# Moving a quarter of the columns of wq's last 64 rows to 64 partitions and eight DMA engines

## The chip, the cores and the metric

The kernel runs on one core of a Trainium2 chip. The metric is the device time of one execution in microseconds (us). The kernel before was timed three times: 210.89, 211.00 and 211.11 us, a median of 211.0 us. A core has five engines that work side by side and wait for each other through semaphores: TensorE (PE: matmuls, and PEld: its weight loads), VectorE (DVE), ScalarE (ACT), GpSimd (POOL) and SyncE (SP). Transfers between the memory of the chip and the core's own memory (128 partitions) are carried by 16 DMA engines. SP, ACT and POOL issue them, each in the order of its own instruction stream.

## The reference: one decode step of attention beside a small MLP

Four sequences (B = 4), one token each, width D = 576. The input x is normalized to xn, and the result is x + A(xn) + B(xn):

```python
q = (x @ wq).reshape(B, Sq, Hq, Dh)             # x [4, 576], wq [576, 4096]: 32 heads of 128
k = k_cache[:, :, Sk - W:, :]                   # 16 kv heads, the last W = 2048 of 8192 positions
v = v_cache[:, :, Sk - W:, :]
p = softmax(q k^T * Dh ** -0.5);  A = (p v).reshape(B, 4096) @ wo            # wo [4096, 576]
x1 = x + hs                                     # hs: gelu(layernorm(x) @ w1), shifted in time, @ w2
B = x1 + gelu(layernorm(x1) @ w3) @ w4          # w3 [576, 4608], w4 [4608, 576]
```

Everything is bfloat16. With a sequence length of 1 every shift of the block with w1 and w2 moves the only token out and a zero in, so hs is zero and the kernel reads neither w1 nor w2. What has to be read is large: the windows of K and V are 32 MiB each, wq, wo, w3 and w4 together some 19 MiB. The arithmetic on it is small, since there are only four tokens.

## The kernel before

**Loads.** The work is cut into eight pairs of kv heads (NPR = 8). For a pair t there is one load of K and one of V, each 128 partitions by 32,768 bytes (4 MiB), issued from POOL (`load_kv`, L125). Three buffers (NKV = 3) hold K and V; a load is issued when the previous user of its buffer is done (`free_one`). Between them POOL issues the four quarters of wo (`load_wo`, L147), w3 in two parts (L152 and L153) and, behind the last V, w4 in six parts (L163), of which the last two are one row of 1,152 bytes per partition. All weights of wq, w3 and w4 share one buffer (tag "w").

**wq.** Its 576 rows are split at 512 (KJ = 4 times 128). The first 512 rows lie four to a partition: `wq_main`, 32,768 bytes on each partition, issued by SP in L143. The last 64 rows lie half a row to a partition: row r is cut into its two halves of 2,048 columns, which go to partitions 2r and 2r + 1, 4,096 bytes on each. SP issues this load first, in L142. ACT issues the load of x (L139), 4 rows of 1,152 bytes. These three are the only loads that SP and ACT issue; everything else is issued by POOL.

**q.** `layernorm` makes xn on four partitions, and `transposed` turns it so that the contracted dimension lies on the partitions: four PE transposes give xnT[:, 0:4] for the first 512 rows. For the last 64 rows POOL first copies the 64 columns of xn into a zeroed tile `dup` (L277 the memset, L279 the copies), once at the even and once at the odd places, and two PE transposes (L284) give xnT[:, 4] and xnT[:, 5], in which every other partition is zero. DVE copies all of it out (L285). So a matmul over 128 partitions with xnT[:, 4 + e] picks half e of the last 64 rows. `q_mm(r, g, j)` (L355) is one such matmul, 512 columns wide, into 32 rows of one of two PSUM tiles; there are 2 x 4 x 5 = 40. The last eight (j = KJ) read the last 64 rows.

**Order.** The schedule is written by hand: each engine works through its instructions in the order in which the program names them. On POOL the issues of the first two K loads (`start_loads`) stand behind the constants, the last of which are sel_jb (L319) and same_j (L329). They need sel_j from DVE (L317), which stands on DVE behind the copy of xnT (L285). On ACT the load of x is followed by a table load and the clearing of xnT, ln2T and qz (`cleared`, L211). Later the loop over pairs mixes scores (L411), softmax and the products with V (L475); at the end PE takes w4 in the order in which it lands (L230, L252), DVE and ACT write out the sum, and SP stores it (L716).

Of the kernel before, what the change touches and what calls it, by code (L numbers as in the profile page):

```python
# [11 lines left out]
BF16 = mybir.dt.bfloat16  # L12
# [10 lines left out]
def kernel(  # L23
# [14 lines left out]
    nc = tc.nc  # L38
    P = 128
    B, Sq, D = A_x.shape  # L40
# [6 lines left out]
    KJ = 4  # L47
    NQ = Hq * Dh
# [4 lines left out]
    QD = 32  # L53
# [8 lines left out]
    NW = SC * QD  # L62
# [15 lines left out]
    wp = ctx.enter_context(tc.tile_pool(name="w", bufs=1))  # L78
# [5 lines left out]
    small = ctx.enter_context(tc.tile_pool(name="small", bufs=2))  # L84
    ps_s = ctx.enter_context(tc.tile_pool(name="ps_s", bufs=3, space=PSUM))
    ps_o = ctx.enter_context(tc.tile_pool(name="ps_o", bufs=2, space=PSUM))
    ps_m = ctx.enter_context(tc.tile_pool(name="ps_m", bufs=2, space=PSUM))
# [49 lines left out]

    x_bf = part(D, B)
    nc.scalar.dma_start(out=x_bf[:], in_=x2)  # L139
    wq_sb = wp.tile([P, KJ * NQ + NQ // 2], BF16, tag="w", name="wq_sb")  # L140
    wq_main = A_wq[0:KJ * P, :].rearrange("(p j) n -> p (j n)", j=KJ)
    nc.sync.dma_start(out=wq_sb[:, KJ * NQ:], in_=A_wq[KJ * P:D, :].rearrange("r (e f) -> (r e) f", e=2))  # L142
    nc.sync.dma_start(out=wq_sb[:, 0:KJ * NQ], in_=wq_main)  # L143

    def load_wo(p):
# [61 lines left out]
    def cleared(shape, name):  # L207
        t = const.tile(shape, BF16, name=name)
        flat = t[:] if len(shape) == 2 else t[:].rearrange("p a b -> p (a b)")
        flat = flat.bitcast(F32)  # L210
        nc.scalar.activation(out=flat, in_=zero[:].bitcast(F32).to_broadcast(list(flat.shape)), func=ACT.Copy)  # L211
        return t

    xnT = cleared([P, KJ + 2, QD], "xnT")
    ln2T = cleared([P, KJ + 2, QD], "ln2T")
    ZP = (NSL - 1) * NJ
    qz = cleared([P, ZP + NPR * 4 * P], "qz")
# [55 lines left out]
                                    op0=ALU.subtract, op1=ALU.mult)  # L273

    def transposed(src_bf, T):
        dup = small.tile([B, 2, P], BF16, tag="dup")
        nc.gpsimd.memset(dup[:], 0.0)  # L277
        for e in range(2):
            nc.gpsimd.tensor_copy(out=dup[:, e, e:P:2], in_=src_bf[:, KJ * P:D])  # L279
        tp = ps_m.tile([P, KJ + 2, B], BF16, tag="m", name="tp")  # L280
        for j in range(KJ):
            nc.tensor.transpose(out=tp[:, j, :], in_=src_bf[:, j:KJ * P:KJ], identity=ident_bf[0:B, 0:B])
        for e in range(2):
            nc.tensor.transpose(out=tp[:, KJ + e, :], in_=dup[:, e, :], identity=ident_bf[0:B, 0:B])  # L284
        nc.vector.tensor_copy(out=T[:, :, 0:B], in_=tp[:])  # L285

    xn_f = part(2 * D, B).bitcast(F32)
    xn_bf = part(D, B)
    layernorm(xn_f, xn_bf, x_bf)
    transposed(xn_bf, xnT)  # L290

    kts = {}
# [9 lines left out]
    for kb in range(NQD):  # L302
        nc.gpsimd.tensor_copy(out=sel[:, :, :, kb, :],
                              in_=ident_bf[:].rearrange("p (ib i e) -> p ib e i", ib=2, e=2))
# [23 lines left out]
    for g in range(2):  # L328
        nc.gpsimd.tensor_copy(out=same_j[:, g * 2 * QD:(g + 1) * 2 * QD].rearrange("p (e s j) -> p e s j", e=2, j=NJ),  # L329
                              in_=sel_j[:].unsqueeze(2).to_broadcast([P, 2, NSL, NJ]))  # L330
# [13 lines left out]
    ln2_bf = part(D, B)  # L344
    layernorm(None, ln2_bf, xn_bf)
    transposed(ln2_bf, ln2T)
    flush_loads()


    q_ps = [ps_s.tile([P, NW], F32, tag="S", name="q_ps") for _ in range(2)]  # L350

    def q_mm(r, g, j):
        c = r * NQD + g
        col, k = (j * NQ + c * NW, j) if j < KJ else (KJ * NQ + g * NW, KJ + r)
        nc.tensor.matmul(out=q_ps[r][g * QD:(g + 1) * QD, :], lhsT=xnT[:, k, :], rhs=wq_sb[:, col:col + NW],  # L355
                         start=(j == 0), stop=False, skip_group_check=True)

    for jr in ((0, 1), (2, 3), (KJ,)):
        for r in range(2):
            for j in jr:  # L360
                for g in range(NQD):
                    q_mm(r, g, j)
# [9 lines left out]
    for r in range(2):  # L372
        nc.vector.tensor_copy(out=q_bf[:, r],  # L373
                              in_=qT_ps[:, r].rearrange("p u (g x) -> p g u x", g=NQD)[:, :, :, 0:B])
    qs_ps = ps_m.tile([P, Hkv, 4, rep, B], F32, tag="m", name="qs_ps")
    for ie in range(4):
        ib, e = divmod(ie, 2)
        nc.tensor.matmul(out=qs_ps[:, :, ie], lhsT=sel[:, ib, e].rearrange("p k i -> p (k i)"),
                         rhs=q_bf.rearrange("p r g u b -> p (r g u b)"), start=True, stop=True)
    for kb in range(NQD):  # L380
        rows = slice(kb * QD, (kb + 1) * QD)
# [365 lines left out]
```

## Time and profile before

| what | value |
|---|---|
| three runs | 210.89, 211.00, 211.11 us |
| the profiled execution's own time | 211.11 us |
| its span, first to last instruction | 209.3 us |
| PE, DVE, ACT, POOL busy | 144.9, 124.8, 29.7, 31.6 us |
| moved by DMA | 87.32 MB in 4,155 packets, 417 GB/s |
| wq main rows: issue to landing | 13.8 us |
| wq last 64 rows: issue to landing | 3.3 us |

The span is what the profiler saw between the first and the last instruction of the core; 1.8 us of the execution lie around it. A "landing" is the moment at which the last part of a transfer has arrived and its semaphore is complete. The trace also holds every DMA packet with its start, its duration, its size and its queue; it does not say on which of the 16 engines a packet ran. Queue q0 is POOL's, q1 is SP's, q10 is ACT's, q8 and q14 bring instructions.

### The profile page before, as it was taken

The numbers are of one execution on the slowest core, as the hardware profiler recorded it, in microseconds if no ns is written. First come the engines' busy times: TensorE is split into PE (matmuls) and PEld (weight loads), VectorE is DVE, ScalarE is ACT, GpSimd is POOL, SyncE is SP. The second block draws the span as 40 slices with busy tenths as digits, with TensorE's granted clock in tenths as the row PEclk, the third lists the DMA queues.
The fourth block names the chain that finished last, engine by engine and source line by source line (L and its number), as shares of the span: only waits on it lengthen the run. The fifth ranks groups of instructions, "written<-read, shape, count | busy, mean of one in ns | idle before, by whom it ended". The sixth has DMA issues, their size and how long they took to land.

```text
span 209.3 us, 2197 instructions
## 1 busy us (share of the span) xinstructions
PE 144.9 (69%) x894; PEld 58.4 (28%) x894; DVE 124.8 (60%) x177; ACT 29.7 (14%) x61; POOL 31.6 (15%) x63
## 2 busy tenths in 40 slices
PE   0249199649679943059996894687957937996954
PEld 0013033222215310014442431143314311443432
DVE  5410779994189700097928990989089818987110
ACT  6402500110102011003001201020002010203100
POOL 5680001003200110000133011001010161100000
PEclk9999859996957995558999999597999996997899
DMA  7999999999999999999999999999999999999991
GB/s 301 401 463 438 401 463 423 438 401 451 451 396 437 447 416 413 392 441 482 413 404 465 432 407 409 477 432 407 457 438 404 446 445 413 438 451 401 419 403 70
DMA packets 4155, 87.32 MB, mean 417 GB/s; under 512 B 488, under 2 KB 496, under 8 KB 1200
## 3 DMA queue, kind: packets, MB, share of 16 engines
q0 software_dynamic: 3840, 82.45, 91.8%
q1 hardware_dynamic: 296, 4.72, 5.4%
q8 instruction: 7, 0.11, 0.2%
q14 instruction: 4, 0.03, 0.0%
q10 hardware_dynamic: 8, 0.00, 0.0%
HBM read 87.17 MB, written 0.00 MB: 416 GB/s over the span
## 4 chain that ended last, share of the span: by engine, by line
DMA 62%; PE 18%; DVE 14%; POOL 2%; issue 2%; ACT 0%; POOLq 0%; DVEq 0%
DMA kn<-in_A_k_cache_dram,row 46%; DMA w_sb<-in_B_w_dram 16%; PE S L411 11%; DVE kt L297 9%; PE O L475 6%; DVE pt L456 1%; POOL w_sb L163 1%; DVE mx L417 1%; PE sum L252 1%; POOL vn L125 0%; PE oT L486 0%; DVE on L496 0%; POOL rstd L268 0%; POOL wo_sb L147 0%; DVE row L116 0%
## 5 line engine op out<-in xcount | busy, mean ns | idle before, releaser
L411 PE MATMUL S<-kt,qz 128*128 128x512 bf16 x256 | 78.4, 439 | 33.4 <-DVE kt L297 33.4
L297 DVE STREAM_TRANSPOSE kt<-kn 128x2048 int32<-128x2048 int32 x32 | 73.7, 2307 | 46.5 <-DMA kn<-in_A_k_cache_dram,row 44.2
L411 PEld LDWEIGHTS <-qz 128*128 128x128 bf16 x256 | 23.4, 104 | 72.6 <-issue 55.8
L475 PE MATMUL O<-vn,pt 128*64 128x512 bf16 x256 | 36.0, 412 | 5.5 <-DVE kt L297 2.5
L456 DVE STREAM_TRANSPOSE pt<-E 64x512 bf16<-64x512 bf16 x32 | 22.1, 690 | 1.2 <-ACT E L447 0.9
L447 ACT ACTIVATE E<-S,bias 128x512 bf16<-128x512 f32 x16 | 10.9, 683 | 75.6 <-DVE bias L440 75.6
L125 POOL DMA_INDIRECT vn<-in_A_v_cache_dram,row x8 | 7.7, 961 | 91.6 <-DVE kt L297 87.5
L475 PEld LDWEIGHTS <-pt 128*64 128x64 bf16 x256 | 13.5, 116 | 22.5 <-issue 13.8
L480 ACT ACTIVATE O_sb<-O,rd 128x512 f32<-128x512 f32 x8 | 5.5, 687 | 62.5 <-PE O L475 62.5
L125 POOL DMA_INDIRECT kn<-in_A_k_cache_dram,row x8 | 7.9, 989 | 42.4 <-PE O L475 23.2
L417 DVE TENSOR_REDUCE mx<-S 128x1 f32<-128x512 f32 x16 | 10.7, 668 | 0.1
L538 PE MATMUL g_ps<-w_sb,ln2T 128*32 128x512 bf16 (+1 forms) x50 | 5.2, 486 | 2.9 <-DMA w_sb<-in_B_w_dram 2.9
L399 PE MATMUL S<-negbig,ohT 4*128 4x512 bf16 x16 | 6.4, 398 | 0.0
L486 PE MATMUL oT<-ident_w,O_sb 128*128 128x128 f32 x32 | 5.2, 286 | 0.0
L355 PE MATMUL q_ps<-wq_sb,xnT 128*32 128x512 bf16 x40 | 4.5, 631 | 0.9 <-DMA wq_sb<-in_A_wq_dram 0.9
L496 DVE TENSOR_REDUCE on<-oT 128x16 bf16<-128x128 f32 x8 | 2.3, 287 | 4.4 <-PE oT L486 4.2
L486 PEld LDWEIGHTS oT<-ident_w,O_sb 128*128 128x128 f32 x32 | 4.1, 149 | 2.2 <-issue 0.9
L163 POOL DMA_DIRECT2D w_sb<-in_B_w_dram x6 | 3.3, 585 | 8.2 <-DMA vn<-in_A_v_cache_dram,row 8.2
L440 DVE TENSOR_SCALAR bias<-bp 128x1 f32<-128x1 f32 x8 | 1.3, 158 | 5.2 <-PE bp L435 5.2
L713 DVE CAST fin<-sum 4x288 bf16<-4x288 f32 x1 | 0.4, 446 | 6.5 <-PE sum L252 6.5
L420 DVE TENSOR_SCALAR dm<-sel_g,mx 128x8 bf16<-128x8 bf16 x16 | 3.9, 243 | 0.6
L373 DVE COPY first<-qT_ps 128x64 bf16<-128x64 bf16 x2 | 0.3, 186 | 6.6 <-PE qT_ps L370 6.6
(103 smaller groups left out, 83.1 us busy)
## 6 DMA issues: line engine op xcount, KB each, us to landing
wo_sb<-in_A_wo_dram POOLq DMA_DIRECT2D x4, 1152.0 KB, 23.6
w_sb<-in_B_w_dram POOLq DMA_DIRECT2D x1, 4608.0 KB, 29.5
wq_sb<-in_A_wq_dram SPq DMA_DIRECT2D x1, 4096.0 KB, 13.8
w_sb<-in_B_w_dram POOLq DMA_DIRECT2D x1, 2592.0 KB, 29.1
w_sb<-in_B_w_dram POOLq DMA_DIRECT2D x2, 576.0 KB, 31.7
w_sb<-in_B_w_dram POOLq DMA_DIRECT2D x1, 1008.0 KB, 31.0
w_sb<-in_B_w_dram POOLq DMA_DIRECT2D x1, 720.0 KB, 32.2
wq_sb<-in_A_wq_dram SPq DMA_DIRECT2D x1, 512.0 KB, 3.3
```

The source lines that it names most:

```text
L125: nc.gpsimd.indirect_dma_start(tl[:].rearrange("p c d -> p (c d)"), None, k_rows if kind == "K" else v_rows, bass.IndirectOffsetOnAxis(ap= ...
L163: nc.gpsimd.dma_start(out=t[:, lo:hi, :], in_=src[e][:, at:at + hi - lo, :])
L297: nc.vector.transpose(out=kt[:], in_=src)
L399: nc.tensor.matmul(out=S_ps[t, u][:].rearrange("p (c k) -> p c k", k=QD), lhsT=ohT[:], rhs=negbig[:].unsqueeze(1).to_broadcast([B, SC, QD] ...
L411: nc.tensor.matmul(out=S_ps[t, u][:], lhsT=qz[:, z0:z0 + P], rhs=kt[:, ib, sl * SC:(sl + 1) * SC, e:2 * QD:2].rearrange("p c k -> p (c k)" ...
L417: nc.vector.reduce_max(out=mx[:], in_=S_ps[t, u][:], axis=AX.X)
L447: nc.scalar.activation(out=E[t, u][:].rearrange("p c k -> p (c k)"), in_=S_ps.pop((t, u))[:], func=ACT.Exp, scale=scale, bias=st["bias", t ...
L456: nc.vector.transpose(out=pts[t % 2 * NU + u][rows, :, e * QD:(e + 1) * QD], in_=e_in[rows])
L475: nc.tensor.matmul(out=O_ps[t][rows], lhsT=pts[t % 2 * NU + u][:, c, :], rhs=vn[:, u, :, c, :], start=(u == 0 and c < 2), stop=False, skip ...
L480: nc.scalar.activation(out=O_sb[t][:], in_=O_ps.pop(t)[:], func=ACT.Copy, scale=st.pop(("rd", t))[:, 0:1])
L486: nc.tensor.transpose(out=oT[:, s, :], in_=o[:, s, :], identity=ident_w[:, s * NJ:s * NJ + P])
L538: nc.tensor.matmul(out=g_ps[g * QD:(g + 1) * QD], lhsT=ln2T[:, k, :], rhs=cols[:, :, i0:i0 + n], start=(j == 0), stop=False, skip_group_ch ...
```

## The change

The four column blocks of 512 in each half row are named by g = 0 to 3. The change takes block g = 0 of both halves, a quarter of the columns of the last 64 rows, out of SP's load. SP's load then has 3,072 bytes on each of the 128 partitions. ACT issues four more loads behind that of x: for each of two blocks of 32 rows (h) and each half (e), 32 partitions by 512 columns (1,024 bytes on a partition). They go to partitions 0 to 63, one row to a partition, so that the two matmuls with g = 0 contract over 64 partitions in place of 128. Within a block, row 8q + g' (q = 0 to 3, g' = 0 to 7) goes to partition 4g' + q, so the outermost dimension of the load has eight steps. xn's 64 columns are put in the same order by a third copy into `dup`, and a third transpose makes xnT[:, 6]. The second use of `transposed` (ln2T) keeps two copies. The tile of wq grows from 18,432 to 18,944 columns, below the 20,736 of w3 and w4 in the same buffer.

```diff
-    wq_sb = wp.tile([P, KJ * NQ + NQ // 2], BF16, tag="w", name="wq_sb")
+    QL = P // 2
+    QT = KJ * NQ
+    QW = NQ // 2 - NW
+    wq_sb = wp.tile([P, QT + QW + 2 * NW], BF16, tag="w", name="wq_sb")
     wq_main = A_wq[0:KJ * P, :].rearrange("(p j) n -> p (j n)", j=KJ)
-    nc.sync.dma_start(out=wq_sb[:, KJ * NQ:], in_=A_wq[KJ * P:D, :].rearrange("r (e f) -> (r e) f", e=2))
+    nc.sync.dma_start(out=wq_sb[:, QT:QT + QW], in_=A_wq[KJ * P:D, :].rearrange("r (e f) -> (r e) f", e=2)[:, NW:])
+    for h in range(2):
+        rows = A_wq[KJ * P + h * QL // 2:KJ * P + (h + 1) * QL // 2, :].rearrange("(q g) n -> g q n", q=4)
+        for e in range(2):
+            nc.scalar.dma_start(out=wq_sb[h * QL // 2:(h + 1) * QL // 2, QT + QW + e * NW:QT + QW + (e + 1) * NW],
+                                in_=rows[:, :, e * NQ // 2:e * NQ // 2 + NW])
     nc.sync.dma_start(out=wq_sb[:, 0:KJ * NQ], in_=wq_main)
...
-    xnT = cleared([P, KJ + 2, QD], "xnT")
+    xnT = cleared([P, KJ + 3, QD], "xnT")
...
     def transposed(src_bf, T):
-        dup = small.tile([B, 2, P], BF16, tag="dup")
+        n = T.shape[1] - KJ
+        dup = small.tile([B, n, P], BF16, tag="dup")
         nc.gpsimd.memset(dup[:], 0.0)
+        if n > 2:
+            nc.gpsimd.tensor_copy(out=dup[:, 2, 0:QL].rearrange("b (h g q) -> b h g q", h=2, q=4),
+                                  in_=src_bf[:, KJ * P:D].rearrange("b (h q g) -> b h g q", h=2, q=4))
...
-        for e in range(2):
+        for e in range(n):
             nc.tensor.transpose(out=tp[:, KJ + e, :], in_=dup[:, e, :], identity=ident_bf[0:B, 0:B])
...
-        col, k = (j * NQ + c * NW, j) if j < KJ else (KJ * NQ + g * NW, KJ + r)
-        nc.tensor.matmul(out=q_ps[r][g * QD:(g + 1) * QD, :], lhsT=xnT[:, k, :], rhs=wq_sb[:, col:col + NW],
+        col, k, rows = (j * NQ + c * NW, j, P) if j < KJ else (QT + (g - 1) * NW, KJ + r, P)
+        if j == KJ and g == 0:
+            col, k, rows = QT + QW + r * NW, KJ + 2, QL
+        nc.tensor.matmul(out=q_ps[r][g * QD:(g + 1) * QD, :], lhsT=xnT[0:rows, k, :], rhs=wq_sb[0:rows, col:col + NW],
                          start=(j == 0), stop=False, skip_group_check=True)
```

More of the change, by code (lines that the diff above doesn't have):

```diff
@@ L275, in transposed @@
     def transposed(src_bf, T):
-        dup = small.tile([B, 2, P], BF16, tag="dup")
+        n = T.shape[1] - KJ
+        dup = small.tile([B, n, P], BF16, tag="dup")
         nc.gpsimd.memset(dup[:], 0.0)
+        if n > 2:
+            nc.gpsimd.tensor_copy(out=dup[:, 2, 0:QL].rearrange("b (h g q) -> b h g q", h=2, q=4),
+                                  in_=src_bf[:, KJ * P:D].rearrange("b (h q g) -> b h g q", h=2, q=4))
         for e in range(2):
             nc.gpsimd.tensor_copy(out=dup[:, e, e:P:2], in_=src_bf[:, KJ * P:D])
-        tp = ps_m.tile([P, KJ + 2, B], BF16, tag="m", name="tp")
+        tp = ps_m.tile([P, KJ + n, B], BF16, tag="m", name="tp")
         for j in range(KJ):
             nc.tensor.transpose(out=tp[:, j, :], in_=src_bf[:, j:KJ * P:KJ], identity=ident_bf[0:B, 0:B])
-        for e in range(2):
+        for e in range(n):
             nc.tensor.transpose(out=tp[:, KJ + e, :], in_=dup[:, e, :], identity=ident_bf[0:B, 0:B])
```

## The prediction

> **What bounds the kernel now.** I read the DMA rows of the page first, then the stretches of time, the end of the chain of waits, and the first nine microseconds of the timeline. The stretches (columns: length, busy time of the five engines, clock, DMA share, GB/s):
>
> ```profile
> 2.00:5.00 3.00, 0.01 (x1) 0.01 (x1) 2.08 (x9) 2.88 (x4) 1.42 (x7) 1.00 1.27 515
> 5.00:14.00 9.00, 3.00 (x18) 1.05 (x18) 3.21 (x12) 2.42 (x3) 6.81 (x17) 1.00 0.95 408
> 14.00:24.00 10.00, 6.35 (x54) 2.81 (x54) 1.82 (x6) 2.42 (x6) 1.60 (x2) 1.00 0.97 419
> 24.00:60.00 36.00, 26.28 (x107) 9.38 (x107) 26.43 (x26) 3.74 (x9) 4.55 (x6) 0.83 1.03 440
> 60.00:172.00 112.00, 82.04 (x477) 32.30 (x476) 69.55 (x90) 12.57 (x29) 13.92 (x20) 0.86 1.00 429
> 172.00:205.00 33.00, 25.77 (x227) 12.21 (x228) 20.45 (x33) 4.58 (x11) 2.10 (x4) 0.90 0.99 421
> ```
>
> The DMA engines are busy everywhere (packets count where they start, hence shares above 1), while no compute engine passes 78% (PE, 25.77 of 33.00 us). The chain ends on them too (columns: start, length, what):
>
> ```profile
> 172.43 33.10 DMA w_sb<-in_B_w_dram
> 205.54 0.04 issue
> 205.58 1.06 PE sum L252 x12
> 206.63 0.43 DVE fin L713
> ```
>
> So the end is set by the last piece of w4, with about 3.8 us behind it (205.5 to 209.3) that the change doesn't touch. A whole K load is 8 packets of 32 KB on each DMA engine, 1.213 us each in the packet records, 9.7 us; from issue to landing K loads take 24.5 us in the median, so some 15 us of work is queued ahead of them. Compute that starts a microsecond late doesn't starve the DMA engines; bytes on the DMA engine that ends last do move the end.
>
> **Which DMA engine ends last.** A packet starts 3 to 4 ns before the end of the one ahead of it on its DMA engine, so the records can be linked into 16 streams; I find no idle time in any between 2 us and the end. All carry the same loads, but they end between 204.20 and 205.90 us. The late ones took code packets: seven of 16,384 B at 0.88 to 0.96 us, four of 8,192 B at 0.31 to 0.49 us. In the first load the streams start one after the other, and x's four packets ran on the first four. I take the first eight to start as the eight that get the new loads. Linked on to the end, with some mix-ups between streams of equal phase, the first eight end at the latest at 205.77 (another linking gives 205.86), the other eight at 205.90.
>
> **The change, part by part.**
>
> *Packets.* Sizes and durations in the records: 4 B 9 ns, 1,152 B 48, 4,096 B 159, 32,768 B 1,213, that is 9 ns plus 1 ns for 27.2 B, less 3.5 ns of overlap. The last 64 rows cost each stream 8 x 155.5 = 1,244 ns now. At 3,072 B the packet is 122 ns, 118.5 net, 8 of them 948: every stream saves 0.30 us. The four loads bring each of eight streams 16 packets of 1,024 B at 46.6 ns, 43.1 net, 690 ns, and four semaphore packets of 5.5, 22 ns: +0.71; if the chip joins them to 4,096 B it is 0.62 + 0.02 = 0.64. So eight streams end 0.34 to 0.42 us later and eight 0.30 earlier. The later of 205.77 + 0.38 = 206.15 and 205.90 - 0.30 = 205.60 is 206.15: **+0.25 us** (0.21 to 0.29; with 205.86 it is 0.30 to 0.38).
>
> *Issues and ACT.* One view of the timeline (start, length, what):
>
> ```profile
> 0.73 0.56 ACTq L139 DMA_DIRECT2D first<-in_A_x_dram  x1
> 0.74 0.40 SPq L142 DMA_DIRECT2D wq_sb<-in_A_wq_dram  x1
> 1.19 0.42 SPq L143 DMA_DIRECT2D wq_sb<-in_A_wq_dram  x1
> 5.07 0.64 POOL L279 COPY dup<-first 4x64 bf16<-4x64 bf16 x2 [0.32 <-DVE first L269]
> 6.05 0.17 DVE L285 COPY xnT<-tp 128x24 bf16<-128x24 bf16 x1 [0.63 <-PE tp L284]
> 6.97 0.27 ACT L310 ACTIVATE ohT<-oh_ps 4x128 bf16<-4x128 f32 x1 [2.09 <-PE oh_ps L308]
> 8.54 1.17 POOL L125 DMA_INDIRECT kn<-in_A_k_cache_dram,row  x1 [0.18 <-issue]
> ```
>
> Four more issues cost ACT 4 x 0.40 (SP's row) to 4 x 0.56 (its own), 1.6 to 2.2 us, ahead of the table load and the clears. ACT stood idle 2.09 us before ohT, and ohT itself comes later by POOL's step below, so this is hidden; xnT's clear moves from 2.62 to at most 4.9, still ahead of DVE's copy at 6.05. Beyond 2.2 us ohT would hold up negbig and sel_j on DVE. SP keeps two issues; its second came 0.45 us after its first, while ACT was issuing x, and nothing shows that one waited for the other. Whether four issues on ACT hold back SP's wq main is not in the trace: 0 to 2.2 us, and I take 0, by that row.
>
> *POOL.* One more copy, 0.25 to 0.47 us (rows of L279), and a memset of 384 in place of 256 elements (0.30, at most 0.45, ending before xn at 4.94): xnT's transposes and copy come 0.25 to 0.47 later. Behind that copy on DVE stand ohk, negbig and sel_j; for sel_j wait sel_jb and same_j on POOL, and behind them the issue of the first K load, at 8.8 to 9.0 in place of 8.54. Its packets start at 13.09 on the first stream, right behind wq main's last, and ahead of wq's semaphore packet, so they were ready by then. How long before, the trace doesn't show: the issue ends at 9.71, so the slack lies between 0 and 3.4 us. Cost: 0 if there is slack, up to 0.47 if there is none; I take 0, since all 16 streams, which leave wq main between 13.09 and 13.45, show the same order without a gap.
>
> *PE.* One more transpose (0.10 load, 0.18 matmul, row L284) under the same 8 us of cover before q_mm at 15.00. Two of 40 q_mm contract over 64 rows: 0 by the row (the moving columns stay 512), at most 0.2 if PE has to empty its array around them. The two late loads on ACT interleave with wq main packet by packet and so land by about 15; their first reader is the 33rd of 40 matmuls (0.11 us each), at 18.6. All of q ends at 23.40 and the first scores wait for the transposed K until 25.84: 2.4 us of cover. If it were gone, the DMA queue's 15 us would be the next one.
>
> Sum: +0.25 on the profiled execution's 211.11 us is 211.36; that execution is the slowest of the three, 0.11 over their median of 211.0, so for a median I predict **211.25 us**.
>
> **A rule weighed.** The chance that this is slower by far rests on small transfers having a fixed price. The row: x, 4.5 KB, held its four DMA engines for packets of 48 to 56 ns and a 9 ns semaphore, and the next load's packets followed. The Trainium skill's page "DMA: Bandwidth & Descriptors", section "Anatomy of one DMA — SWDGE (gpsimd) path", gives about 2.0 us fixed plus bytes / 436 GB/s per DMA, and its "Rules for kernel authors" calls transfers under 64 KB mostly overhead and advises against splitting by partition halves. By that, an estimate, four loads of 32 KB in sequence are 8.3 us; only if the streams stood still meanwhile would the time be 219. The same page lets such a load run on the lowest-numbered eight DMA engines, and gives partitions 0 to 63 to eight of them; no row here shows the numbers.
>
> **Rivals.**
>
> 1. *The relieved eight set the end* (faster). If the late streams are all in the half that loses packets, or my first eight are the wrong eight, the end moves by up to -0.30: 210.7. For it: the latest stream, 205.90, is in that half. Against: the 16 KB code packet at 32.7 us, when the linking is still sure, lies in the first eight, and its stream ends at 205.59; 205.59 + 0.34 is already above 205.90. It decides only if the loaded half ends before 205.5.
> 2. *The first K load comes too late* (slower). No slack at 13.09: every stream idles for what POOL's copy adds, and no stream is spared, since the relieved ones stand 0.30 longer: up to +0.47, or 211.5. It decides from a slack under 0.2 us. If, instead, ACT's issues hold back wq main, the relieved streams run dry at about 3.0 us and wait up to 1.4 (1.19 + 1.03, the latency of SP's first issue, + 2.2 = 4.4): -0.3 + 1.4 = +1.1, 212.1. Against both: the rows above.
> 3. *One more code packet* (slower). ACT and POOL get longer; a further 8 or 16 KB on a late stream adds 0.31 to 0.96, so 211.6 to 212.2.
> 4. *The loads spread over all 16* (not what the change says): 8 packets each, 0.345 + 0.02 - 0.30, +0.07: 211.05.
>
> **How the numbers follow.** A measurement of this kernel can tell about 0.2% (0.42 us) from no change: 210.58 to 211.42. The forecast, +0.1 to +0.45, has 0.55; rival 1 0.12; rival 2 0.20; rival 3 0.08; rival 4 and others 0.05. Slower by over 0.2%: the forecast's upper end (0.09 of its 0.55; the runs alone scatter by 0.1), most of rival 2 (0.17), rival 3 (0.08) and 0.02: 0.36. Faster: rival 1's end with scatter, 0.05, and 0.01. Same: the rest, 0.58. The range runs from 210.75, within rival 1, to 211.9, between rival 2's two prices. The forecast's own is 211.1 to 211.45.
>
> **What would show it.** Right: the packets of 3,072 and 1,024 B at some 122 and 47 ns; q10's bytes up by 0.13 MB and q1's down by as much; the last w4 landing about 0.25 us later against the start of the first load; xnT's copy at 6.3 to 6.5; q still done by 24; DMA shares as above. Wrong: a gap in the packets at 3 to 4 or at 13 us, an eighth code packet of 16 KB, or an end that moves forward because the late streams were the relieved ones.

## The result, and the profile after

The changed kernel took 212.12 us (median of six runs, 211.76 to 212.33) against 210.9 us for the kernel before (six runs beside it, 210.78 to 211.11): a ratio of 1.0056, 95% interval 1.0045 to 1.0066. That is 1.2 us slower. The forecast was 211.25, with 211.9 as the upper end of its range. Its profiled execution took 212.04 us, 0.93 more than the one before. Executions that were disturbed and some per cent longer are left out of every ratio; the profiled ones of `extra_eight` and `extra_sixteen` below (220.66 and 229.18 us) were such, so only the ratios of these two are used.

The packets are what the change says (queues of the profile page: packets, MB, share of 16 engines' span):

```profile
DMA packets 4315, 87.32 MB, mean 415 GB/s; under 512 B 520, under 2 KB 656, under 8 KB 1360
q1 hardware_dynamic: 296, 4.59, 5.3%
q10 hardware_dynamic: 168, 0.14, 0.2%
```

The bytes are the same 87.32 MB; 0.13 MB have gone from SP's queue q1 to ACT's q10, in 128 packets of 1,024 B (median 46 ns) and 32 more semaphore packets. SP's tail packets (the last 64 rows) are 3,072 B and 121 ns at the median. These terms of the forecast (122 and 46.6 ns) hold to about a nanosecond. The timeline of the start, as far as the matmuls of q (start, length, engine and line), shows what it did not have:

```profile
0.74 0.56 ACTq L139 DMA_DIRECT2D first<-in_A_x_dram  x1
1.34 2.90 ACTq L149 DMA_DIRECT2D wq_sb<-in_A_wq_dram  x4
4.27 1.28 ACT L219 ACT_TABLE_LOAD   x1 [4.27 <-issue]
6.41 0.17 DVE L297 COPY xnT<-tp 128x28 bf16<-128x28 bf16 x1 [0.90 <-PE tp L296]
7.86 0.27 ACT L322 ACTIVATE ohT<-oh_ps 4x128 bf16<-4x128 f32 x1
8.16 0.18 DVE L324 TENSOR_SCALAR negbig<-oh_ps 4x32 bf16<-4x32 f32 x1 [1.30 <-ACT ohT L322]
9.43 1.17 POOL L125 DMA_INDIRECT kn<-in_A_k_cache_dram,row  x1 [0.18 <-issue]
14.91 5.71 PE L369 MATMUL q_ps<-wq_sb,xnT 128*32 128x512 bf16 x40
```

The four issues held ACT for 2.90 us, 0.72 each with the gaps between them (0.68 at the median without). The forecast had 0.40 to 0.56 each and a limit of 2.2 us. ohT carries no wait any more: ACT itself is late. It starts at 7.86 in place of 6.97, DVE's negbig and sel_j follow, and so the first K load is issued at 9.43, 0.89 us later than before. POOL's share of this is what the forecast said: xnT's copy at 6.41, 0.36 late. The chain of waits (start, length, what) now runs through these issues from the start:

```profile
3.56 0.68 ACTq L149
4.24 0.03 issue
4.27 1.28 ACT L219
...
6.03 1.81 ACT qz L219
7.84 0.03 issue
7.86 0.28 ACT ohT L322
...
9.43 15.44 DMA kn<-in_A_k_cache_dram,row
...
172.72 33.71 DMA w_sb<-in_B_w_dram
206.47 1.07 PE sum L260 x12
```

The last wait is still w4's, at 206.43 in place of 205.54. Another place to look is the stretch from 13 to 16 us, where wq main ends and K begins. In the trace of before (length, busy time of the five engines, clock, DMA share, GB/s):

```profile
13.00:16.00 3.00, 2.03 (x20) 1.01 (x22) 0.45 (x2) 0.00 (x0) 2.15 (x5) 1.00 1.22 524
```

The same stretch in the trace of after:

```profile
13.00:16.00 3.00, 2.73 (x22) 0.96 (x26) 0.59 (x2) 0.00 (x0) 2.24 (x7) 1.00 1.05 413
```

The same stretch in `sixteen`, one of the experiments below:

```profile
13.00:16.00 3.00, 1.79 (x18) 0.67 (x18) 0.59 (x2) 0.00 (x0) 2.25 (x6) 1.00 1.00 428
```

The DMA share fell from 1.22 to 1.05 and the rate from 524 to 413 GB/s, but this by itself does not show idle DMA engines: a packet counts where it starts, and a stretch of 3 us holds the starts of two or three packets of 1.2 us per stream. `sixteen` has an even lower share, 1.00, and no idle stream there. What shows that streams ran dry is the time between the packets, summed over the 16 streams (below: 3.15 us after, 0 before).

**Where the time went, by streams.** The packets of the trace after can be linked into 16 streams as before; now the 1,024 B packets mark the loaded eight. The loaded ones end at the latest at 206.73, the relieved ones at 206.16. The forecast's linking of the trace before had 205.77 and 205.90 for the two halves, so the halves moved by +0.96 and +0.26 where the forecast had +0.38 and -0.30. The difference between these two moves, 0.70, is the forecast's 0.68. Both are some 0.57 later than forecast, and three sums over the 16 streams give that amount:

- the first 32 KB packet of wq main took 1,475 ns in the mean, before 1,236: 0.24 us per stream. Main started 0.35 earlier (2.97 against 3.32; 0.32 in the mean over the streams) and its last packets ended no earlier (13.14 to 13.50 against 13.09 to 13.45). The rest of those 0.32 us went to the 38 small packets that left ahead of 13 us, 0.10 per stream in the mean, which the forecast had counted.
- the streams idled 3.15 us in all between 13 and 16 us, one of them 0.98, before 0: 0.20 us per stream.
- the first 16 packets of K took 1,334 ns in the mean, before 1,214: 0.12 us per stream.

Together 0.56 us. The last landing moved by 0.83 us (205.89 to 206.72, the start of the last semaphore packet), about 0.25 + 0.57. This is an account by means over 16 streams in two executions; what each part costs alone is for the experiments.

### The profile page after: what moved, and what is told of

Read it like the earlier page. It is cut to its first block, busy times and chain, and to the rows that moved or that the text cites. A ratio compares the mean times of both kernels' runs of the same rounds, so it can differ in the third digit from the quotient of the medians.

```text
span 210.3 us, 2208 instructions
## 1 busy us (share of the span) xinstructions
PE 145.2 (69%) x895; PEld 58.6 (28%) x895; DVE 124.7 (59%) x177; ACT 29.8 (14%) x61; POOL 31.9 (15%) x64
## 2 busy tenths in 40 slices
DMA packets 4315, 87.32 MB, mean 415 GB/s; under 512 B 520, under 2 KB 656, under 8 KB 1360
## 4 chain that ended last, share of the span: by engine, by line
DMA 62%; PE 15%; DVE 10%; issue 7%; ACT 2%; POOL 2%; ACTq 2%; POOLq 0%; DVEq 0%
DMA kn<-in_A_k_cache_dram,row 46%; DMA w_sb<-in_B_w_dram 16%; PE S L425 8%; DVE kt L309 7%; PE O L489 6%; ACTq L149 1%; DVE pt L470 1%; ACT qz L219 1%; POOL w_sb L171 1%; ACT L219 1%; DVE mx L431 1%; PE sum L260 1%; POOL vn L125 0%; DVE on L510 0%; POOL wo_sb L155 0%
## 5 line engine op out<-in xcount | busy, mean ns | idle before, releaser
L425 PE MATMUL S<-kt,qz 128*128 128x512 bf16 x256 | 77.1, 433 | 34.4 <-DVE kt L309 34.4
L489 PE MATMUL O<-vn,pt 128*64 128x512 bf16 x256 | 37.1, 422 | 5.9 <-DMA vn<-in_A_v_cache_dram,row 5.3
L489 PEld LDWEIGHTS <-pt 128*64 128x64 bf16 x256 | 14.7, 118 | 22.5 <-issue 14.2
L369 PE MATMUL q_ps<-wq_sb,xnT 128*32 128x512 bf16 (+1 forms) x40 | 5.7, 622 | 0.0
L294 PE MATMUL tp<-ident_bf,first 4*128 4x4 bf16 x8 | 0.6, 173 | 5.1 <-DVE first L277 5.1
```

The source lines that it names most:

```text
L425: nc.tensor.matmul(out=S_ps[t, u][:], lhsT=qz[:, z0:z0 + P], rhs=kt[:, ib, sl * SC:(sl + 1) * SC, e:2 * QD:2].rearrange("p c k -> p (c k)" ...
L489: nc.tensor.matmul(out=O_ps[t][rows], lhsT=pts[t % 2 * NU + u][:, c, :], rhs=vn[:, u, :, c, :], start=(u == 0 and c < 2), stop=False, skip ...
```

## The experiments

Theory D: ACT's issues make the first K load late, the streams run dry, and most of the loss comes from there. Theory U: the loaded streams are 0.4 us longer, and nothing else. Theory R: wq main's first packets are slowed by ACT's loads. Below, "stream-us" are microseconds summed over the 16 streams; 16 of them are 1 us on every stream. The plain length of a 32 KB packet is 1,213 ns.

### ACT late, nothing else

`act_late`, on the kernel before; `act_later` has two of the first line and one of 2,400.

```diff
     qz = cleared([P, ZP + NPR * 4 * P], "qz")
+    nc.scalar.activation(out=qz[:, 0:4120].bitcast(F32), in_=zero[:].bitcast(F32).to_broadcast([P, 2060]), func=ACT.Copy)
+    nc.scalar.activation(out=qz[:, 0:2200].bitcast(F32), in_=zero[:].bitcast(F32).to_broadcast([P, 1100]), func=ACT.Copy)
```

> The kernel before with ACT kept busy by two more clears of qz, about 2.9 us in all, as long as the four issues took; no load is moved, POOL and PE have nothing more to do. Theory D: ohT at about 7.8, the first K issue at about 9.4 us, gaps at 13 to 14 us and +0.4 to +0.9 us. U and R: no change.

> The dose to the run with ACT 2.9 us late: the kernel before with three more clears of qz on ACT, about 4.9 us. First K issue at about 11.5 in place of 8.54 us, 2.0 us later than in that run. Theory D, no slack left: 2.0 us more, in all +2.4 to +3.2 us, with some 30 or more stream-us of gaps at 13 to 16 us. If the DMA streams catch up later, or the +0.85 came from the clears themselves: about as before, +0.5 to +1.2.

`act_late`: 1.0038 (1.0025 to 1.0051), +0.8 us. Two clears on ACT, and no byte moved, cost two thirds of what the change costs. Its timeline (start, length, what):

```profile
6.87 1.12 ACT L219 ACTIVATE qz<-zero 128x1100 f32<-128x1100 f32 x1
8.01 0.27 ACT L312 ACTIVATE ohT<-oh_ps 4x128 bf16<-4x128 f32 x1
9.58 1.17 POOL L125 DMA_INDIRECT kn<-in_A_k_cache_dram,row  x1 [0.18 <-issue]
```

This is what D expected; U and R expected no change. But the dose fails: `act_later`, with the K issue another 2.03 us later, is at 1.0048 (1.0030 to 1.0067), +1.0 us, not +2.4 to +3.2. That is the range noted for the other outcome, in which the streams catch up later or the clears themselves cost the time. Its timeline:

```profile
10.05 0.27 ACT L313 ACTIVATE ohT<-oh_ps 4x128 bf16<-4x128 f32 x1
11.61 1.17 POOL L125 DMA_INDIRECT kn<-in_A_k_cache_dram,row  x1 [0.18 <-issue]
```

Here the first K packet starts at 13.48, 1.9 us after its issue, while wq main's last packets end at 13.05 to 13.51. So the packets are there 1.9 us after the issue at the earliest, on streams that run dry; in `k_early_after` below, behind 32 KB packets of wq main, they came 4.5 us after it. The loss is not the delay passed on. It has two parts: streams that idle between 13 and 16 us (0.85 stream-us in `act_late`, 7.7 in `act_later`) and first K packets that are longer (1,403 and 1,784 ns in the mean, against 1,214). The mean landing of the first K load over the streams moves by 0.40 and 1.05 us. For `act_later` that is the whole +1.0 us, for `act_late` half of its +0.8; which streams are hit could decide the rest, but no run shows it. No run parts ACT's delay from the late K load: the one with ACT late and K early, `k_early_after`, has a greater loss of another kind.

Why the first K packets are long stays open. They are not those of the streams that idled longest: in `act_later` the two that idled 1.48 us each have the shortest, 1,220 and 1,279 ns.

### The K load early, and the loads on SP

`k_early_after` and `k_early_before`, the same move on both kernels:

```diff
-    start_loads()
-
     xsum = xn_f
...
+    start_loads()
     sel_jb = const.tile([P, 2 * NJ], BF16)
```

> The changed kernel, with the issue of the first two K loads on POOL ahead of sel_jb and same_j, so that it no longer stands behind ACT's ohT; about 7.0 us in place of 9.43 us. Theory D (the late first K load leaves the DMA streams idle at 13 to 14 us, 3.1 stream-us, and most of the +1.2 us comes from there): idle time gone, +0.2 to +0.5 us over the kernel before. Theory U (the eight streams with the 16 small packets are simply 0.4 us longer, and nothing else): the delay of K costs nothing, still +1.0 to +1.3. Theory R (wq main's first packets are slowed by ACT's loads, 3.2 against 0.9 stream-us over their plain duration at 3 to 5 us): still +0.9 or more.

> The control: the kernel before with the same move on POOL, first K issue at about 6.7 in place of 8.54 us. The streams had no idle time there, so D, U and R all expect no change within 0.2 us; K's packets will mix with wq main's, wq lands 1 to 3 us later, and its cover of 2.4 us may go without an effect on the end. If it is faster by more than 0.2 us, the first K load was late in the kernel before already.

`loads_on_sp`, on the changed kernel:

```diff
+    nc.sync.dma_start(out=wq_sb[:, 0:KJ * NQ], in_=wq_main)
     for h in range(2):
...
-            nc.scalar.dma_start(out=wq_sb[h * QL // 2:(h + 1) * QL // 2, QT + QW + e * NW:QT + QW + (e + 1) * NW],
+            nc.sync.dma_start(out=wq_sb[h * QL // 2:(h + 1) * QL // 2, QT + QW + e * NW:QT + QW + (e + 1) * NW],
                                 in_=rows[:, :, e * NQ // 2:e * NQ // 2 + NW])
-    nc.sync.dma_start(out=wq_sb[:, 0:KJ * NQ], in_=wq_main)
```

> The changed kernel with the four loads issued by SP behind wq main, so ACT is as early as before. What is left of the delay of the first K issue is POOL's third copy and the larger memset, 0.36 us, so about 8.9 us. Theory D: +0.4 to +0.8 us, between the two kernels. Theory U: unchanged, +1.0 to +1.3, since the bytes per stream are the same. Theory R: wq main's first packets as fast as before, +0.3 to +0.6.

The control is 1.0001 (0.9988 to 1.0013): an early K load neither helps nor hurts the kernel before. The other two missed by far. `k_early_after` is 1.034 (1.0308 to 1.0372), 7 us slower, and `loads_on_sp` 1.0502 (1.0462 to 1.0541), 11 us. The timeline of `k_early_after` (start, length, what) tells why, and two of its stretches (length, busy time of the five engines, clock, DMA share, GB/s):

```profile
16.25 3.61 PE L368 MATMUL q_ps<-wq_sb,xnT 128*32 128x512 bf16 x32 [2.77 <-DMA wq_sb<-in_A_wq_dram]
24.13 1.15 PE L368 MATMUL q_ps<-wq_sb,xnT 64*32 64x512 bf16 x4 [4.27 <-DMA wq_sb<-in_A_wq_dram]
30.26 1.15 PE L368 MATMUL q_ps<-wq_sb,xnT 64*32 64x512 bf16 x4 [4.99 <-DMA wq_sb<-in_A_wq_dram]
```

```profile
24.00:44.00 20.00, 11.10 (x41) 3.94 (x42) 8.54 (x8) 4.13 (x8) 0.00 (x0) 1.00 1.02 438
44.00:60.00 16.00, 13.56 (x67) 5.11 (x67) 15.52 (x18) 1.45 (x4) 2.49 (x4) 1.00 0.70 283
```

The 64-row matmuls waited for their small loads until 24 and 30 us. q came 11 us later than in the changed kernel, the first K buffer was freed late (the next K load was issued at 45.87 us against 35.63), and at 44 to 60 us the streams idled 66 stream-us of 256, a quarter. The small packets were late because a stream serves its queues in turn, one packet each. The records of one loaded stream of the changed kernel (start and length in ns, bytes, queue):

```
5666    46   1024 q10
5708  1213  32768 q1
6917    46   1024 q10
6960  1213  32768 q1
8169    46   1024 q10
8211  1213  32768 q1
```

One small packet leaves per 1.25 us. The Trainium skill says the same in "DMA: Bandwidth & Descriptors", section "Queues, rings and completion order": an engine takes turns between the queues that have work for it, packet by packet. So 16 small packets behind 32 KB packets take some 20 us. In the changed kernel 89 of the 128 small packets left between 13.0 and 14.2 us, with hardly a 32 KB packet between them, because K was late. The late K load that costs it part of its 1.2 us is also what spares it the 7 us. `loads_on_sp`, where the small packets stand behind wq main in SP's own queue, shows the same with the K issue only 0.34 late:

```profile
8.88 1.17 POOL L125 DMA_INDIRECT kn<-in_A_k_cache_dram,row  x1 [0.18 <-issue]
14.36 3.60 PE L369 MATMUL q_ps<-wq_sb,xnT 128*32 128x512 bf16 x32
26.56 1.15 PE L369 MATMUL q_ps<-wq_sb,xnT 64*32 64x512 bf16 x4 [8.60 <-DMA wq_sb<-in_A_wq_dram]
32.76 1.15 PE L369 MATMUL q_ps<-wq_sb,xnT 64*32 64x512 bf16 x4 [5.05 <-DMA wq_sb<-in_A_wq_dram]
```

Its wq main also began with long packets (1,348 ns in the mean), though ACT issued nothing but x. Theory R falls: it is not ACT's loads that lengthen them.

### Two loads, on 16 and on eight DMA engines

`sixteen` (g, q = 16, 4) and `two_loads` (8, 8), on the changed kernel, with the copy into `dup` in the same order:

```diff
-    for h in range(2):
-        rows = A_wq[KJ * P + h * QL // 2:KJ * P + (h + 1) * QL // 2, :].rearrange("(q g) n -> g q n", q=4)
-        for e in range(2):
-            nc.scalar.dma_start(out=wq_sb[h * QL // 2:(h + 1) * QL // 2, QT + QW + e * NW:QT + QW + (e + 1) * NW],
-                                in_=rows[:, :, e * NQ // 2:e * NQ // 2 + NW])
+    rows = A_wq[KJ * P:D, :].rearrange("(q g) n -> g q n", q=4)
+    for e in range(2):
+        nc.scalar.dma_start(out=wq_sb[0:QL, QT + QW + e * NW:QT + QW + (e + 1) * NW],
+                            in_=rows[:, :, e * NQ // 2:e * NQ // 2 + NW])
```

> The changed kernel with the moved quarter in two loads of 64 partitions over 16 DMA engines in place of four over eight: 8 packets of 1,024 B on every stream, two issues on ACT, no uneven spread. The sum of D and U says: two issues hold ACT for 0.8 to 1.5 us, less than its 2.09 us of idle time, the first K issue at 8.9, a small gap at most, +0.07 us for the bytes: 0 to +0.4 us. If the third copy, the 64-row matmuls or the small packets as such cost the +1.2: +0.8 or more. If the small packets alternate with the 32 KB packets of the K loads and land after some 20 us, q is late and the time is +1 or more with gaps behind 24 us, as in the two runs that were 7 and 11 us slower.

> The changed kernel with the moved quarter in two loads of 64 partitions on eight DMA engines: bytes per stream as in the changed kernel (16 small packets on eight streams), but two issues on ACT, so the first K load is issued at about 8.9 in place of 9.43 us. If the gap at 13 to 14 us were the whole cost: +0.3 to +0.5. If the gap is what lets the small packets out ahead of K: with the gap gone the 16 packets alternate one for one with 32 KB packets, land at 24 to 30 us, q starves the loop, and the time is +5 us or more.

`sixteen`: 1.0036 (1.0022 to 1.0051), +0.8 us, above its range for D and U and in that for a price of the third copy, the 64-row matmuls or the small packets as such. Its timeline:

```profile
1.34 1.25 ACTq L148 DMA_DIRECT2D wq_sb<-in_A_wq_dram  x2
7.32 0.27 ACT L321 ACTIVATE ohT<-oh_ps 4x128 bf16<-4x128 f32 x1 [1.12 <-PE oh_ps L319]
8.88 1.17 POOL L125 DMA_INDIRECT kn<-in_A_k_cache_dram,row  x1 [0.18 <-issue]
```

ACT waits again before ohT, the K issue is 0.34 late, and no stream idles at 13 to 16 us; K's first packets have their plain 1,213 ns. That K was in time here does not show slack by itself, since wq main's last packets ended 0.33 us later in the mean than in the kernel before. In `loads_on_sp`, with the same K issue, they ended at 12.85 to 13.28 and the streams idled only 0.1 stream-us, though its small packets filled part of the gap. So 0.34 us of delay costs next to nothing, and the 0.89 of the changed kernel is not free. The loss of `sixteen` is earlier: 1.5 stream-us of idle time between 5 and 13 us, and, behind the first 16, 32 KB packets of wq main that take 4.3 stream-us more than their plain length (1,252 ns in the mean). So the small packets beside wq main cost something even without uneven streams and without a late K load.

`two_loads` was 1.0067 (1.0052 to 1.0081), +1.4 us, between its two ranges, with times from 212.2 to 214.3 us. In its profiled execution (214.26 us) x landed late and the K issue was at 9.36, not 8.9, so it does not part the two outcomes; its second small load was read only at 27.58 us, and q starved the loop as in the runs above, less (26 stream-us of idle time at 44 to 60 us).

### The split alone

`split_128`, on the kernel before: the last 64 rows in two loads over all 128 partitions.

```diff
-    nc.sync.dma_start(out=wq_sb[:, KJ * NQ:], in_=A_wq[KJ * P:D, :].rearrange("r (e f) -> (r e) f", e=2))
+    tail = A_wq[KJ * P:D, :].rearrange("r (e f) -> (r e) f", e=2)
+    nc.sync.dma_start(out=wq_sb[:, KJ * NQ + NW:], in_=tail[:, NW:])
+    nc.scalar.dma_start(out=wq_sb[:, KJ * NQ:KJ * NQ + NW], in_=tail[:, 0:NW])
```

> The kernel before with the last 64 rows of wq in two loads over all 128 partitions and all 16 streams, 3,072 B by SP and 1,024 B by ACT: the split alone, with even streams, one issue on ACT (0.4 us) and no third copy, so the first K load is as early as before. D and U: 0 to +0.2 us (one more packet per row, 0.04 us x 8 less what the shorter packets save, +0.05 in all). If small packets beside wq main are the cost: +0.4 or more.

1.0028 (1.0016 to 1.0041), +0.6 us: above D's and U's range, and in that for a cost of small packets beside wq main. With even streams, one issue on ACT of 0.36 us and the K issue at 8.53, splitting the load costs something by itself. wq main's first packets took 1,422 ns in the mean, long as in all kernels with the shorter tail. The rest can't be read well: the profiled execution was one of the longer ones (212.53 against a median of 211.47), and one stream was five microseconds behind in wq.

### More bytes on eight streams

`extra_eight` and `extra_sixteen` (without the rearrange), on the kernel before: a load that nobody reads, into columns by which wq's tile is widened.

```diff
+    nc.sync.dma_start(out=wq_sb[0:P // 2, KJ * NQ + NQ // 2:], in_=A_wq[0:P // 2, 0:NQ // 2].rearrange("(q g) n -> g q n", g=8))
```

> The kernel before with one more load that nobody reads: 64 partitions by 4,096 B of wq, issued by SP behind wq main, in an order that puts it on eight DMA engines, 8 packets of 4,096 B (8 x 155.5 = 1.24 us) on each. It isolates the uneven part. Theory U (the end is that of the last stream): the loaded eight end at 205.77 + 1.24 = 207.01 in place of 205.90, so +1.1 us (+0.9 to +1.3). If only the mean over 16 streams counts: +0.6.

> The same bytes as extra_eight, but with the plain order of rows, which spreads them over 16 DMA engines, 4 packets of 4,096 B on each (0.62 us). Every theory: +0.6 us (+0.4 to +0.8). What extra_eight has beyond this is the price of the uneven spread.

`mid_eight` and `mid_sixteen` (without the rearrange), on the kernel before, with loads into a tile of their own, and `mid_eight_own`, which replaces the two loads by eight of 32 partitions:

```diff
+        if t == 5:
+            nc.scalar.activation(out=spare[:, 0:2], in_=ident_bf[:, 0:2], func=ACT.Copy)
+            nc.sync.dma_start(out=spare[:], in_=A_wq[0:P, 0:NW].rearrange("(q g) n -> g q n", g=8))
+            nc.sync.dma_start(out=spare[:], in_=A_wq[0:P, 0:NW].rearrange("(q g) n -> g q n", g=8))
```

> The kernel before with two more loads that nobody reads, issued by SP in the middle of the kernel (at t = 5, some 110 us in): each 128 partitions by 1,024 B of wq in an order of eight steps, so 16 packets of 1,024 B on eight streams, the very packets that the change adds to eight streams, twice over. The start of the kernel is untouched. Theory U (the last stream ends the kernel): 32 x 43 ns = 1.4 us on eight streams, 205.77 + 1.4 = 207.2 against 205.9: +1.1 to +1.4 us. If only the mean over the 16 streams counts: +0.7. If small packets between the 32 KB packets are dearer than their own length: more than +1.5.

> The same two loads in the plain order of rows, 8 packets of 1,024 B each on all 16 streams: 16 x 43 = 0.7 us on every stream, +0.6 to +0.8 us by every theory that prices packets by their length. The difference to mid_eight is the price of the uneven spread, +0.5 to +0.7 by theory U, 0 otherwise.

> As the run with two mid-kernel loads on eight streams (+2.9 us, in which the 32 KB packets of all streams grew by 25 stream-us), but cut as the changed kernel cuts its loads: eight loads of 32 partitions by 1,024 B, so that a stream writes only partitions that it also writes for K and V. Again 32 packets of 1,024 B on eight streams, 1.4 us. Theory U with plain lengths: +1.1 to +1.4 us and 32 KB packets as long as in the kernel before. If mixing small with large packets is dear by itself: +2 us or more and long 32 KB packets again.

| run | ratio (95%) | difference, us | expected by lengths, us |
|---|---|---|---|
| extra_eight | 1.0124 (1.0109 to 1.0139) | +2.6 | +1.1 |
| extra_sixteen | 1.0089 (1.0075 to 1.0104) | +1.9 | +0.6 |
| mid_eight | 1.0131 (1.0114 to 1.0148) | +2.8 | +1.1 to 1.4 |
| mid_sixteen | 1.0051 (1.0036 to 1.0066) | +1.1 | +0.6 to 0.8 |
| mid_eight_own | 1.0342 (1.0317 to 1.0367) | +7.2 | +1.1 to 1.4 |

Each pair says that eight streams are dearer than sixteen at the same bytes, by 0.7 and 1.7 us, and each single run costs more than its lengths. In the `mid` runs the excess is in the 32 KB packets that directly follow a small one on their stream: in `mid_eight_own` 236 such packets took 22.8 us more than their plain length, 0.10 each, in `mid_sixteen` 222 took 3.1 us, 0.014 each. On eight streams the 22.8 us are 2.9 us each; with 1.4 of lengths this is 4.3 of the 6 us by which that execution was longer, so part of `mid_eight_own` is unexplained. Keeping each stream to its own partitions, as it does, did not prevent the long packets. Nor is eight against sixteen the whole of it: at the start of the kernel such packets were 0.01 us longer in `k_early_after`, with small packets on eight streams, and 0.03 in `sixteen`. What does it is open. In the changed kernel this hardly occurs: 45 such packets, 0.4 us together.

### The changed kernel once more

`changed_again` is the changed kernel as it is.

> The changed kernel itself, beside the others on one chip. D and U added: 0.7 to 0.85 from the late first K load, 0.3 to 0.4 from the uneven streams, in all +1.0 to +1.3 us. The loaded streams (those with the 1,024 B packets) hold the latest end.

1.0048 (1.0029 to 1.0067), +1.0 us, beside `act_later` and the `mid` runs. The K issue was at 9.44, the streams idled 3.0 us in all at 13 to 16 us, and wq main's and K's first packets took 1,379 and 1,411 ns. So what the trace of after shows at the start comes again. Whether the loaded streams hold the latest end, as expected, was not settled: the linking has mix-ups by then.

## Why the prediction was wrong, point by point

- **What bounds the kernel.** Right. The DMA streams set the end: the last landing of w4 moved by 0.83 us, the profiled execution by 0.93.
- **Packets and uneven streams.** Right in size: 121 and 46 ns, 16 small packets on eight streams, a difference of 0.70 us between the halves (forecast 0.68), and the loaded half ends last.
- **"Every stream saves 0.30 us."** This term failed. The shorter tail let wq main start 0.32 us earlier in the mean, but its first packets grew by 0.24, so that most of the saving was gone. The profiled executions with the shorter tail all show this (1,348 to 1,475 ns in seven runs, against 1,227 to 1,249 in the seven with the old tail and no other load behind wq main: before, `act_late`, `act_later`, `k_early_before` and the three `mid` runs). The cause is not known. Main's first packets begin at 3.07 to 3.19 us in the mean in the first seven and at 3.39 to 3.54 in the others, so the earlier start as such is a candidate beside the shape of the tail, and no run parts the two.
- **Issues and ACT.** This step failed too, and by more: "so this is hidden". An issue was priced at 0.40 to 0.56 us, from issues of other shapes, and measured 0.72 with its gap; `mid_eight_own`'s issues of the same shape on SP took 0.68 at the median, as on ACT without the gaps. The four held ACT past the end of its idle time, ohT came 0.89 us late (0.35 in `sixteen`, where two issues took 1.25), and the first K load with it. By the packets this cost 0.32 us (0.20 of idle streams and 0.12 of long K packets), the greater part of what the forecast missed; `act_late`, with no other part of the change, lost 0.8 us. The forecast named the consequence ("beyond 2.2 us ohT would hold up negbig and sel_j") and then did not give its price a chance of its own. The section "Issuing engines are not separate DMA queues" of the Trainium skill's page "DMA: Bandwidth & Descriptors" calls the time of an issue usually small relative to the transfer; here 2.90 us of issues stand against 0.7 us of packets on each loaded stream.
- **POOL and the slack of the first K load.** The delay by POOL was right (0.36, forecast 0.25 to 0.47), and 0.34 us of it costs next to nothing, as `loads_on_sp` shows. The statement that it costs nothing was right for that step alone; with ACT's it came to 0.89, which is not free, and the gap at 13 us, which the prediction had named as a sign of being wrong, was there.
- **PE.** The two late loads "land by about 15": they did (last packet at 15.4, semaphore packet at 16.8), but the reason given was wrong. Only 38 of the 128 small packets got through beside wq main; the others got through in the gap that the late K load left. With K in time they land at 24 to 32 us and the cover of 2.4 us and the queue's 15 us are both used up, which `k_early_after` and `loads_on_sp` paid with 7 and 11 us. That was luck, and this rival was not in the prediction at all.
- **Rival 2 and the sum.** Rival 2 happened, through ACT rather than POOL alone, and beside the forecast's mechanism, not in its place. The prediction treated them as alternatives: +0.25 or up to +0.47. Added they are more than either: by the packets 0.25 + 0.32 for the late K load + 0.24 for wq main's first packets = 0.81, against the 0.83 by which the last landing moved. The range stopped at 211.9 for that reason. That this sum closes does not prove it. Tested alone, a late ACT cost 0.8 us and the split 0.6; with the 0.25 forecast for the uneven spread that is more than the 1.2 us of the change. And `sixteen`, without the late K load and the uneven spread, still lost 0.8. So the parts do not simply add, and how they share the 1.2 us stays open.
- **Rivals 1, 3 and 4.** Not seen: the relieved streams do not set the end, there are again seven 16 KB code packets, and the small packets lie on eight streams. The price of 2.0 us per load under "A rule weighed" is given for loads issued by GpSimd, while these were issued by ACT; nothing like its 219 us came.

## What to carry to other kernels

Take the price of an issue from a row of its own shape; where no such row exists, follow the engine's order past the point at which its idle time is used up, and give that branch its own chance. Add mechanisms that lie on different stretches of the same stream; they are not alternatives. Before giving a small load to a busy set of DMA streams, count its packets per stream and multiply by the large packet that alternates with each (here 16 times 1.25 us): that is about when it lands.

## What the runs showed of the hardware that was not expected

- A load of 32 partitions in an order of eight steps took 0.68 us to issue at the median, on ACT as on SP. Loads over 128 partitions in the plain order took 0.33 to 0.42, in an order of eight steps 0.60 and 0.75 (`mid_eight`), and 64 partitions in an order of 16 steps 0.61 (`sixteen`).
- Where the first K load was issued at 9.36 us or later, its first packets took 1,334 to 1,784 ns in the mean in place of 1,214. In the changed kernel the long ones are mostly not on the streams that waited: eight that began K at 13.97 to 14.16 us have 1,213 to 1,271 ns, while six of the seven that began by 13.50, directly behind wq main, have 1,325 to 1,538.
- A 32 KB packet that follows a 1,024 B packet on its stream took 0.01 to 0.10 us longer in the mean with small packets on eight streams (`k_early_after`, `mid_eight_own`), and 0.014 to 0.03 us with small packets on all 16 (`mid_sixteen`, `sixteen`).
- POOL's indirect load had its first packets running 1.9 us after the start of its issue on idle streams, and 4.5 us after it (7.46 to 11.92 in `k_early_after`) behind 32 KB packets of another queue.
